# A polynomial-sketch attention and feed-forward kernel: its program rewritten as small named steps in a given order, with cheaper weight conversion, plain-maximum rounding grids and the first block's numerators ahead of its normalisation

## The chip, the core and the metric

The kernel runs on one core of a Trainium2 chip. The metric is the device time of one execution in microseconds (us), as the median of several runs. The program before takes 302.24 us (three runs, 301.96 to 303.37). The profile of one execution spans 299.0 us from its first to its last instruction.

A core has five engines that run their own instruction streams and wait for each other through semaphores. PE (TensorE) multiplies matrices and writes to PSUM, [...]. DVE (VectorE) and ACT (ScalarE) do elementwise work and copy results out of PSUM. POOL (GpSimd) does a little elementwise work on SBUF. SP (SyncE) issues the DMA transfers.

## The reference, cut to what matters

```python
def phi(x):                                   # x: (4, 4, 1088, 32)
    a = einsum('rd,bhsd->bhsr', S1, x)        # r = 8
    b = einsum('rd,bhsd->bhsr', S2, x)
    return outer(a, b).reshape(..., 64)
kv  = einsum('bhsf,bhsd->bhfd', phi(k), v)
z   = sum(phi(k), axis=2)
num = einsum('bhsf,bhfd->bhsd', phi(q), kv)
den = einsum('bhsf,bhf->bhs', phi(q), z) + 1e-6
x   = (num / den) laid out as (4352, 128)
out = ((x @ w1) * (x @ w2)) @ w3 @ w_out      # w1, w2: 128 x 1024, w3: 1024 x 1024, w_out: 1024 x 128
```

The denominator can come near zero, so it needs more than single precision. Both kernels get it from split numbers: a leading part rounded to a coarse grid plus a rest. They don't sum phi(k). They build the Gram matrix `G = k' k` (32 x 32 for each head), from it `T = G S1`, from it `N = P T` with `P = S2' S2`, and the denominator of a row is the product of its `a = q S1` and its `y = q N`. The sketch matrices and the four weights arrive as float64, as pairs of 32-bit words, and are converted to float32 on the chip. Both kernels use `w3o = w3 @ w_out`, computed once, so that each group of 512 rows needs three products for each of eight 128-column blocks c: a, b and o.

## The kernel before

It is a list of closures, merged by estimated costs. A weight is converted in chunks of 512 columns, with float64 words `lo` and `hi`:

```python
def words():                                   # ACT
    nc.scalar.mul(x["c"], hi.bitcast(F32), 2.0 ** -112)
    nc.scalar.mul(x["m"].bitcast(I32), lo.bitcast(U32), 2.0 ** -29)
    if signs:                                  # w1, w2 only
        x["s"] = zeros_with_signs(x["c"], 128, CW)
def join():                                    # DVE
    if signs:
        nc.vector.scalar_tensor_tensor(t, c, 3, x["s"], ALU.logical_shift_left, ALU.bitwise_or)
    else:
        nc.vector.tensor_scalar(t, c, 3, 0x7FFFFFF8, ALU.logical_shift_left, ALU.bitwise_and)
        nc.vector.scalar_tensor_tensor(t, c, -(1 << 31), t, ALU.bitwise_and, ALU.bitwise_or)
def add():                                     # DVE
    nc.vector.tensor_tensor(x["t"], x["t"], x["m"].bitcast(I32), ALU.add)
```

A rounding grid is the row maximum, cut to a power of two and scaled; then it is added and subtracted:

```python
def to_grid(m, bits):                          # two small DVE instructions for each grid
    nc.vector.tensor_scalar(mi, mi, 0x7F800000, None, ALU.bitwise_and)
    nc.vector.tensor_scalar(m, m, 1.5 * 2.0 ** (24 - bits), None, ALU.mult)
```

A batch b of k gives Gram and value sums that share one bank (`kvz`), and the rows past 1024 are a separate small set of products for pairs of batches. After them come G, T and N, each a product of split numbers (`pair_mm`, three matmuls). A half batch of q goes through these steps:

```python
# grid_q, lead_q (ACT, two passes), rest_q (POOL, or DVE where lean), ay1 and ay2 (a and y, PE), split, dens, dens2, phi ...
nc.vector.tensor_mul(bs, C, 1 / den)           # dens2: b is divided by the denominator
nc.vector.tensor_mul(ph, a x bs)               # phi: outer products, 128 x 1024
# phT: 8 PE transposes (L807), 2 ACT copies; nd: two matmuls with kv (L818); ACT copy to xT (L822)
```

The feed-forward of group g, block c:

```python
a_ps = psum.tile([128, 512], F32, tag="h", bufs=3)
nc.tensor.matmul(a_ps, w1[:, cols], xT[key])                     # L862
nc.scalar.copy(a_sb, a_ps)                                       # L864
b_ps = psum.tile([128, 512], F32, tag="h", bufs=3)
nc.tensor.matmul(b_ps, w2[:, cols], xT[key])                     # L866
nc.vector.tensor_mul(ab, a_sb, b_ps)                             # L868
nc.tensor.matmul(o_ps[g], w3o[:, c], ab, ...)                    # L875
```

The first part is written out in a fixed order, with 88 idle matmuls on zeros (L215) in it. From group 1 on, the streams are merged:

```python
run(merge(ffn_steps(1, 16), k_steps(1), w_out))
run(merge(ffn_steps(None, 4), q_main(1, 0)))
run(merge(ffn_steps(2, 6), q_main(1, 1), rest_steps(1) + k_steps(2)))
# ... cut ...
run(merge(ffn_steps(7, 6), q_rest()))
run(ffn_steps(8, 2))
```

Of the kernel before, what the change touches and what calls it, by code (L numbers as in the profile page):

```python
# [15 lines left out]
U32 = mybir.dt.uint32  # L16
I64 = mybir.dt.int64
# [4 lines left out]
EPS = 1e-6  # L22
CW = 512
LAG = 16
NRAW = 6


def bview(t, free):

    return bass.AP(tensor=t.tensor, offset=t.offset, ap=[list(t.ap[0])] + [list(d) for d in free])  # L30


@with_exitstack
def kernel(
    ctx: ExitStack,
    tc: tile.TileContext,
    q: bass.AP,
    k: bass.AP,
    v: bass.AP,
    S1: bass.AP,  # L40
    S2: bass.AP,
    moe_w1: bass.AP,
    moe_w2: bass.AP,
    moe_w3: bass.AP,
    moe_w_out: bass.AP,
    out: bass.AP,
):

    nc = tc.nc
    B, H, S, D = q.shape
    r = S1.shape[0]
    assert (B, H, S, D, r) == (4, 4, 1088, 32, 8)
    DM, DF = moe_w1.shape
    assert DM == H * D == 128 and DF % CW == 0  # L60
    NC = DF // 128
    NJ = S // 128
    SM = NJ * 128
    SR = S - SM
    HD = H * D
    NT = S // 32
    assert SR == 64 and NT * 32 == S
    KM = H * NJ * D

    consts = ctx.enter_context(tc.tile_pool(name="consts", bufs=1))  # L70
    io = ctx.enter_context(tc.tile_pool(name="io", bufs=2))
    work = ctx.enter_context(tc.tile_pool(name="work", bufs=2))
    psum = ctx.enter_context(tc.tile_pool(name="psum", bufs=1, space=bass.MemoryType.PSUM))

    def load_main(t, src, b):
        nc.sync.dma_start(t.rearrange("p h c d -> p h (c d)"),
                          bass.AP(tensor=src.tensor, offset=b * H * S * D,
                                  ap=[[NJ * D, 128], [S * D, H], [1, NJ * D]]))

    def load_rest(t, src, m):
        for i in range(2):  # L90
            nc.sync.dma_start(t[i * SR:(i + 1) * SR],
                              bass.AP(tensor=src.tensor, offset=((2 * m + i) * H * S + SM) * D,
                                      ap=[[D, SR], [S * D, H], [1, D]]))

    k_sb, v_sb, k_rs, k_all = {}, {}, {}, {}
    by_head = {}

    def load_in(which, b):


        src, held = {"k": (k, k_sb), "v": (v, v_sb)}[which]
        if which == "k":
            t = io.tile([128, KM + HD], F32, tag="k", name="k_sb")
            k_all[b] = t if b % 2 == 0 else t[:, :KM]
            held[b] = t[:, :KM].rearrange("p (h c d) -> p h c d", h=H, c=NJ)
        else:
            held[b] = io.tile([128, H, NJ, D], F32, tag=which, name=which + "_sb")
        if which == "v" and b:
            for t in range(4):
                nc.sync.dma_start(held[b][t * 32:(t + 1) * 32].rearrange("p h c d -> p h (c d)"),  # L110
                                  bass.AP(tensor=v.tensor, offset=b * H * S * D + t * NJ * D,
                                          ap=[[32 * D, 32], [S * D, H], [1, NJ * D]]))
        else:
            load_main(held[b], src, b)
        if which == "k" and b % 2 == 0:
            k_rs[b // 2] = t[:, KM:].rearrange("p (h d) -> p h d", h=H)
            load_rest(k_rs[b // 2], k, b // 2)

    def load_by_head(which, b):
        n = {"q": NT, "k": 32}[which] * D  # L120
        t = io.tile([128, n], F32, tag=which + "h", bufs={"q": 2, "k": 1}[which], name=which + "h")
        if which == "q":
            nc.sync.dma_start(t, bass.AP(tensor=q.tensor, offset=b * H * S * D, ap=[[n, 128], [1, n]]))
        else:
            for h in range(H):
                nc.sync.dma_start(t[h * 32:(h + 1) * 32],
                                  bass.AP(tensor=k.tensor, offset=(b * H + h) * S * D, ap=[[n, 32], [1, n]]))
        by_head[which, b] = t

    def natural(t, half):  # L130

        n = work.tile([128, 4, H, D], F32, tag="w3c", bufs=3, name="nat")
        nc.scalar.copy(n, bview(t[:, 0, 4 * half], [[D, 4], [NJ * D, H], [1, D]]))
        return n.rearrange("p c h d -> p c (h d)")

    qT_rest = consts.tile([128, B * SR], F32, tag="qT_rest")
    v_rs = [consts.tile([128, H, D], F32, tag=f"vr{m}", name=f"vr{m}") for m in range(2)]

    w1 = consts.tile([DM, DF], F32, tag="w1")
    w2 = consts.tile([DM, DF], F32, tag="w2")  # L140
    wo = consts.tile([128, NC, DM], F32, tag="wo")
    w3o = consts.tile([128, NC, DM], F32, tag="w3o")

    def chunk_src(name, i):
        if name == "wo":
            n = CW // DM
            return bass.AP(tensor=moe_w_out.tensor, offset=moe_w_out.offset + i * n * 128 * DM,
                           ap=[[DM, 128], [DM * 128, n], [1, DM]])
        if name == "w3":
            ko, half = divmod(i, DF // CW)  # L150
            return moe_w3[ko * 128:(ko + 1) * 128, half * CW:(half + 1) * CW]
        src = moe_w1 if name == "w1" else moe_w2
        return src[:, i * CW:(i + 1) * CW]

    NH = DF // CW
    chunks = [(w, i) for i in range(NH) for w in ("w1", "w2")]
    chunks += [("wo", i) for i in range(NC * DM // CW)] + [("w3", i) for i in range(NC * NH)]
    raw, n_raw = {}, [0]

    def load_raw(n):  # L160
        while n_raw[0] < min(n, len(chunks)):
            i = n_raw[0]
            n_raw[0] += 1
            raw[i] = io.tile([128, CW], I64, tag="raw", bufs=NRAW, name="raw")
            if i == 2:

                nc.vector.memset(raw[i].bitcast(I32)[:1, :1], 0)
            src = chunk_src(*chunks[i])
            dst = raw[i]
            if len(src.shape) == 3:  # L170
                dst = dst.rearrange("p (c d) -> p c d", d=DM)
            nc.sync.dma_start(dst, src)

    s_raw = consts.tile([r, 2, D], I64, tag="s_raw")
    for i, x in enumerate((S1, S2)):
        nc.sync.dma_start(s_raw[:, i], x)
    load_in("k", 0)
    load_in("v", 0)
    load_by_head("q", 0)
    load_rest(v_rs[0], v, 0)  # L180
    load_raw(2)

    def load_more():
        load_raw(NRAW)
        load_in("k", 1)
        load_by_head("k", 1)
        load_in("v", 1)
        load_by_head("q", 1)
        load_rest(v_rs[1], v, 1)

# [3 lines left out]
    make_identity(nc, ident)  # L194
    mask4 = consts.tile([128, H], F32, tag="mask4")
    mask2 = consts.tile([128, 2], F32, tag="mask2")
    for t in (mask4, mask2):
        nc.vector.memset(t, 0.0)
    for h in range(H):
        nc.vector.memset(mask4[h * D:(h + 1) * D, h:h + 1], 1.0)  # L200
        nc.vector.memset(mask2[h * D:(h + 1) * D, h % 2:h % 2 + 1], 1.0)
    mask4n = consts.tile([128, H], F32, tag="mask4n")
    nc.vector.tensor_scalar(mask4n, mask4, -1.0, None, ALU.mult)
    mask_blk = bview(mask4, [[1, H], [0, D]])
    first_act = consts.tile([1, 1], F32, tag="first_act")
    nc.scalar.copy(first_act, mask4[:1, :1])


    zeros = consts.tile([128, 256], BF16, tag="zeros")
    nc.vector.memset(zeros, 0.0)  # L210
    idle_ps = psum.tile([128, CW], F32, tag="out", name="idle_ps")

    def idle(times, n=256):
        for _ in range(times):
            nc.tensor.matmul(idle_ps[:, :n], zeros[:, :128], zeros[:, :n], start=True, stop=True)  # L215
    idle(24)
    sgn = [consts.tile([128, CW], I32, tag=f"sgn{i}", name=f"sgn{i}") for i in range(2)]
    for t in sgn:
        nc.vector.memset(t, 0)

    def halves(words, n):

        w = words.bitcast(I32)
        return bview(w, [[2, n]]), bview(w[:, 1:], [[2, n]])

    def zeros_with_signs(c, p, n):

        sgn.append(sgn.pop(0))  # L230
        t = sgn[0][:p, :n]
        nc.scalar.copy(bview(t.bitcast(F16)[:, 1:], [[2, n]]), c)
        return t

    def split_words(lo, hi, p, n):


# [10 lines left out]
        def parts():  # L248
# [4 lines left out]
            return a.bitcast(F32), m  # L253
        return words, parts

    def convert(n, dst, signs=True):

        x = {}
# [741 lines left out]
```

## Time and profile before

| what | value |
|---|---|
| time, median of three | 302.24 us |
| span of the profile | 299.0 us |
| first feed-forward matmul starts | 34.04 us |
| last matmul (the transposes of the last output) ends | 295.45 us |
| feed-forward matmuls a, b, o | 212 us of PE busy time |
| feed-forward on DVE (product a times b) | 47.1 us |
| bytes moved by DMA | 22.37 MB |

The page gives for each engine how long it had an instruction in work (busy), and the same cut into 40 slices. The matmul of a float32 operand has two records in the trace, so 72 products show as 144. The groups of instructions tell what one instruction of a kind and shape takes, and a table of windows gives the busy time of each engine in a stretch of the span. The chain of waits follows the last instruction back to what released it.

In the first 20 us PE is busy for 16.93 us, but many of these matmuls are the idle ones. From 80 to 280 us PE is busy in practically all of the time.

### The profile page before, as it was taken

The page shows a single profiled execution, that of the slowest core. Times are in us where ns is not written, and L with a number is a line of the kernel's source. Part 1 is how long each engine was busy: PE and PEld are TensorE (multiplying, and loading weights), DVE is VectorE, ACT ScalarE, POOL GpSimd, SP SyncE. Part 2 cuts the span into 40 slices and gives each one's busy share as a digit, 9 for nine tenths or more (in the row PEclk, how much of TensorE's full clock was granted, in tenths as well). Part 3 has the DMA queues.
Part 4 walks back from the last instruction along what each step waited for, and adds up shares of the span by engine and source line. Part 5 has one row for each costly group of instructions (what it writes and reads, how often), then busy time and mean ns, then how long its engine had stood idle before and what let it go on. Part 6 is the DMA issues. An engine that isn't in the chain of part 4 may idle for free.

```text
span 299.0 us, 5582 instructions
## 1 busy us (share of the span) xinstructions
PE 282.7 (95%) x2214; PEld 159.8 (53%) x2214; DVE 207.6 (69%) x523; ACT 117.1 (39%) x226; POOL 7.5 (3%) x12
## 2 busy tenths in 40 slices
PE   7987799589999999999999999999999999999994
PEld 5876343267767774545644435464444444444572
DVE  6989779999998985699579329864862583453131
ACT  4634665667886322320242322122423323223122
POOL 0000000000000010010010001000100000000000
PEclk9999999979999999999999999999999999999999
DMA  5649996456744002200100200020002002002020
GB/s 164 211 99 311 254 309 252 134 160 201 246 123 134 0 2 35 71 2 10 30 0 0 35 2 1 2 37 0 2 0 35 2 0 35 1 2 35 0 35 18
DMA packets 28729, 22.37 MB, mean 75 GB/s; under 512 B 20000, under 2 KB 25248, under 8 KB 28704
## 3 DMA queue, kind: packets, MB, share of 16 engines
q1 hardware_dynamic: 28704, 22.03, 26.8%
q8 instruction: 17, 0.28, 0.4%
q14 instruction: 8, 0.07, 0.1%
HBM read 19.80 MB, written 2.23 MB: 74 GB/s over the span
## 4 chain that ended last, share of the span: by engine, by line
PE 80%; DVE 11%; ACT 3%; DMA 2%; issue 1%; SPq 1%; DVEq 0%
PE ps_o L875 19%; PE a_ps L862 19%; PE b_ps L866 18%; PE ps_kvz L557 5%; PE ps_w3o L428 5%; PE ps_x L818 3%; PE ps_wt L421 2%; PE ps_c L725 2%; PE ps_ph L807 2%; DMA k_sb<-in_k_dram 1%; DMA raw<-in_moe_w_dram 1%; PE ps_ab L504 1%; DVE g_k L301 1%; DVE w3c L285 1%; PE ps_c L738 1%
## 5 line engine op out<-in xcount | busy, mean ns | idle before, releaser
L868 DVE TENSOR_TENSOR ab<-ffa,b_ps 128x512 f32<-128x512 f32 (+1 forms) x72 | 47.1, 655 | 64.7 <-PE b_ps L866 62.9
L864 ACT COPY ffa<-a_ps 128x512 f32<-128x512 f32 (+1 forms) x72 | 40.4, 562 | 98.1 <-PE a_ps L862 98.0
L862 PE MATMUL a_ps<-xT,w 128*128 128x512 f32 (+1 forms) x144 | 71.9, 581 | 1.0 <-ACT xT L822 0.7
L866 PE MATMUL b_ps<-xT,w 128*128 128x512 f32 (+1 forms) x144 | 70.3, 570 | 0.0
L875 PE MATMUL ps_o<-ab,w3o 128*128 128x512 f32 (+1 forms) x144 | 70.0, 582 | 0.1
L866 PEld LDWEIGHTS b_ps<-xT,w 128*128 128x128 f32 x144 | 27.2, 190 | 30.1 <-issue 24.9
L875 PEld LDWEIGHTS ps_o<-ab,w3o 128*128 128x128 f32 x144 | 25.3, 189 | 23.9 <-issue 21.6
L862 PEld LDWEIGHTS a_ps<-xT,w 128*128 128x128 f32 x144 | 24.9, 190 | 23.5 <-issue 14.3
L809 ACT COPY pT<-ps_ph 128x512 f32<-128x512 f32 (+1 forms) x18 | 9.2, 565 | 21.0 <-PE ps_ph L807 21.0
L428 PEld LDWEIGHTS ps_w3o<-wo,w3T 128*128 128x128 f32 x128 | 16.5, 205 | 1.5 <-issue 1.2
L428 PE MATMUL ps_w3o<-wo,w3T 128*128 128x128 f32 x128 | 17.0, 289 | 0.0
L269 ACT ACTIVATE cv_c<-raw 128x512 f32<-128x512 f32 x22 | 14.9, 679 | 2.9 <-DVE w3c L282 1.5
L270 ACT ACTIVATE cv_m<-raw 128x512 int32<-128x512 uint32 x22 | 15.0, 681 | 1.8 <-DVE w3c L285 1.5
L421 PE MATMUL ps_wt<-ident,w3c 128*128 128x128 f32 x64 | 10.2, 288 | 4.7 <-DVE w3c L285 4.7
L215 PE MATMUL idle_ps<-zeros 128*128 128x256 bf16 x88 | 12.7, 309 | 1.7 <-DVE zeros L210 1.7
L822 ACT COPY xT<-ps_x 128x512 f32<-128x512 f32 (+1 forms) x9 | 5.1, 563 | 19.0 <-PE ps_x L818 19.0
L421 PEld LDWEIGHTS ps_wt<-ident,w3c 128*128 128x128 f32 x64 | 7.5, 147 | 8.7 <-ACT cv_c L269 4.2
L215 PEld LDWEIGHTS <-zeros 128*128 128x128 bf16 x88 | 9.6, 112 | 3.8 <-DVE zeros L210 1.7
L701 POOL TENSOR_TENSOR q<-qT,q 128x512 f32<-128x512 f32 x5 | 5.9, 1183 | 208.6 <-ACT q L697 208.6
L423 ACT COPY w3T<-ps_wt 128x512 f32<-128x512 f32 x16 | 9.2, 585 | 4.9 <-PE ps_wt L421 4.6
L807 PEld LDWEIGHTS ps_ph<-ident,ph 128*128 128x128 f32 x68 | 7.9, 142 | 5.8 <-issue 4.0
L285 DVE CUSTOM_DVE_ANT_0 w3c<-w3c,cv_m 128x1024 uint16<-128x1024 uint16 x16 | 10.8, 682 | 0.0
(182 smaller groups left out, 343.9 us busy)
## 6 DMA issues: line engine op xcount, KB each, us to landing
raw<-in_moe_w_dram SPq DMA_DIRECT2D x20, 512.0 KB, 5.0
qh<-in_q_dram SPq DMA_DIRECT2D x4, 544.0 KB, 5.8
k_sb<-in_k_dram SPq DMA_DIRECT2D x4, 512.0 KB, 5.2
out_dram<-oT SPq DMA_DIRECT2D x32, 64.0 KB, 1.9
kh<-in_k_dram SPq DMA_DIRECT2D x12, 128.0 KB, 6.4
v_sb<-in_v_dram SPq DMA_DIRECT2D x12, 128.0 KB, 5.1
raw<-in_moe_w_out_dram SPq DMA_DIRECT2D x2, 512.0 KB, 7.7
v_sb<-in_v_dram SPq DMA_DIRECT2D x1, 512.0 KB, 4.9
```

The lines of the kernel that those rows point to most:

```text
L215: nc.tensor.matmul(idle_ps[:, :n], zeros[:, :128], zeros[:, :n], start=True, stop=True)
L269: nc.scalar.mul(x["c"], hi.bitcast(F32), 2.0 ** -112)
L270: nc.scalar.mul(x["m"].bitcast(I32), lo.bitcast(U32), 2.0 ** -29)
L421: nc.tensor.transpose(ps[:, c], w3c[i][:, c * 128:(c + 1) * 128], ident)
L428: nc.tensor.matmul(ps, w3T[ko][:, c], wo[:, c], start=(c == 0), stop=(c == NC - 1))
L557: nc.tensor.matmul(out[h * D:(h + 1) * D], lhs, rhs, start=start, stop=stop, skip_group_check=True)
L807: nc.tensor.transpose(ps[:, j * 128:(j + 1) * 128], s["ph"][:, j, 2 * p:2 * p + 2].rearrange("p h i j -> p (h i j)"), ident)
L862: nc.tensor.matmul(a_ps[:, :n], w1[:, cols], xT[key], start=True, stop=True)
L864: nc.scalar.copy(a_sb[:, :n], a_ps[:, :n])
L866: nc.tensor.matmul(b_ps[:, :n], w2[:, cols], xT[key], start=True, stop=True)
L868: nc.vector.tensor_mul(ab[:, :n], a_sb[:, :n], b_ps[:, :n])
L875: nc.tensor.matmul(o_ps[g][:, :n], w3o[:, c], ab_sb.pop((g, c))[:, :n], start=c == 0, stop=c == NC - 1)
```

## The change

The whole program is cut into named steps, and one list gives the order in which all of them are issued, so each engine's own order follows from it. The changes in the work itself:

- A weight is converted in tiles of 1024 columns. The float32 magnitude is built in one DVE instruction, and the low bits and the sign, which ACT writes as the two 16-bit halves of one word, are joined in one addition.
- A grid is the maximum itself times a power of two, no longer cut to a power of two. The scaling happens inside the instruction that adds, so the two small instructions are gone.
- Rows past 1024 are a ninth chunk of k and v, with zeros in the other half of the partitions. The value sums have a bank of their own and no longer share that of the Gram sums. G, T and N take two matmuls for each product.
- The first 512 rows of q form their outer products and numerators from the undivided b, before N is there. The denominator divides the numerators, which are then transposed. Only this first block does so.
- Only the first two blocks of q take the form with few large matmuls for a and y (before: three). The rest of q is subtracted on DVE instead of POOL; for batch 0 POOL forms the outer products of k.
- 24 idle matmuls instead of 88. The buffers of `ab` go from 18 to 17, those of k, v and q from two to one each.

```diff
-        nc.scalar.mul(x["c"], hi.bitcast(F32), 2.0 ** -112)
-        nc.scalar.mul(x["m"].bitcast(I32), lo.bitcast(U32), 2.0 ** -29)
+    act.mul(x["c"], halves(raw[n], 1024)[1].bitcast(F32), 2.0 ** -112)                                   # step w.c
+    act.copy(bview(sign_bits[n % 2].bitcast(F16)[:, 1:], [[2, 1024]]), x["c"])                           # step w.s
+    act.mul(bview(sign_bits[n % 2].bitcast(U16), [[2, 1024]]), halves(raw[n], 1024)[0].bitcast(U32), 2.0 ** -29)  # w.m
-            nc.vector.tensor_scalar(t, c, 3, 0x7FFFFFF8, ALU.logical_shift_left, ALU.bitwise_and)
-            nc.vector.scalar_tensor_tensor(t, c, -(1 << 31), t, ALU.bitwise_and, ALU.bitwise_or)
-        nc.vector.tensor_tensor(x["t"], x["t"], x["m"].bitcast(I32), ALU.add)
+    dve.tensor_scalar(x["d"].bitcast(I32), c, 3, 0x7FFFFFF8, ALU.logical_shift_left, ALU.bitwise_and)    # step w.j
+    dve.tensor_tensor(d, d, sign_bits[n % 2], ALU.add)                                                   # step w.a
 ... cut ...
-        nc.vector.tensor_scalar(mi, mi, 0x7F800000, None, ALU.bitwise_and)
-        nc.vector.tensor_scalar(m, m, 1.5 * 2.0 ** (24 - bits), None, ALU.mult)
+        eng.scalar_tensor_tensor(dst, m, 2.0 ** (24 - bits), x, ALU.mult, ALU.add)
+        eng.scalar_tensor_tensor(dst, m, -2.0 ** (24 - bits), t, ALU.mult, ALU.add)
 ... cut ...
-                ps = psum.tile([128, 128], F32, tag="kvz", name="ps_kvz")
+                    a["g"] = ps("kvz", [128, 2 * D], "ps_g")
+                    a["kv"] = ps("out" if b == 0 else "t", [128, 64], "ps_kv")
 ... cut: first block of q (kind "A") ...
+            bsrc = s["Cb"].rearrange("p j (h i) -> p (j h) i", i=r) if cut else s["bs"]
+                        pe.matmul(o[:, j, 64 * p:64 * (p + 1)], s["pT"][:, p, j * 128:(j + 1) * 128],
+                                  kz[b][:, 64 * p:64 * (p + 1)], start=True, stop=True)
+                dve.tensor_mul(s["xs"]..., s["x"]..., bview(s["rc"], [[1, nj * H], [0, D]]))
+                    pe.transpose(cols(t, j), s["xs"][:, j], ident)
 ... cut: the order, its first part ...
+ORDER = """
+s.load c.mask k0.zero k0.load1 k0.load0 k0.loadr s.zero c.ident kr0.load q0.load s.words kr1.load s.pair w1.load
+s.split k0.nat0 kh1.load kr0.tr s.lead k0.tr0 s.T k0.kT0 k0.max0 kr0.kT k0.nat1 s.blk k0.g0 q0.tr kr0.ab kr1.tr
 ... cut ...
+k0.N1 q0.sca k0.kv0 k0.Na w0.m k0.kv1 k0.Nb k0.kvr k0.Nf k0.Nh k0.Nl q0.C1 k0.kvm w0.j q1.l2 k0.kzt q0.A1 warm0
+q0.smy w3.c q0.al q0.sty q0.C1t q0.shy q0.phi q1.l1 k0.kz q0.sly q0.pt0 q0.scy q0.p01 q0.pt1 q0.pc0 q0.p2 q1.A0
+w0.a q0.pc1 q0.x q0.p12 q1.rm q0.dn q1.C0 q0.de w1.j q0.rc q0.xs w1.a q0.xt q0.xT w3.j w3.s g0.0a q0.restT
 ... cut ...
```

In the step names, k0 is batch 0 of k, q0 and q1 are the first two blocks of q, w0 and w1 hold the first and second half of w1 and w2, w2 is w_out, w3 to w10 are w3, f is the fold of w3 and w_out, and g is the feed-forward with its steps a, c (copy), b, m (product) and o.

## The prediction

> **What bounds the kernel now.** I read the page's shares first, then the slices, then a table of windows, and last the groups of instructions.
>
> ```profile
> PE 282.7 (95%) x2214; PEld 159.8 (53%) x2214; DVE 207.6 (69%) x523; ACT 117.1 (39%) x226; POOL 7.5 (3%) x12
> ...
> PE   7987799589999999999999999999999999999994
> ```
>
> PE is busy for 95% of the span, but the slices show where it isn't: the first 60 us and the last slice. From the ninth slice on it never pauses. The windows (us; busy of PE, weight loads, DVE, ACT, POOL; granted clock; DMA) put numbers to that:
>
> ```profile
> 20.00:34.00 14.00, 11.01 (x84) 8.22 (x84) 13.07 (x39) 6.63 (x11) 0.00 (x0) 1.00 1.03 272
> 34.00:42.00 8.00, 7.46 (x32) 4.10 (x32) 5.40 (x13) 6.14 (x11) 0.00 (x0) 1.00 1.10 271
> 42.00:60.00 18.00, 14.10 (x41) 5.95 (x40) 16.95 (x35) 11.46 (x21) 0.00 (x0) 1.00 0.63 227
> 60.00:80.00 20.00, 18.66 (x206) 14.34 (x206) 19.08 (x33) 15.34 (x29) 0.00 (x0) 0.91 0.65 191
> 80.00:115.00 35.00, 34.91 (x352) 25.15 (x349) 32.11 (x93) 18.28 (x35) 1.16 (x1) 1.00 0.25 76
> ...
> 280.00:299.00 19.00, 14.74 (x57) 10.12 (x55) 3.67 (x8) 3.58 (x9) 0.00 (x0) 1.00 0.10 21
> ```
>
> So there are three stages. In the **head**, up to the first feed-forward matmul at 34.04 us, the chain of waits runs mostly through DVE (13.07 of 14 us busy). In the **conversion stage**, 34 to 80 us, PE idles 0.54 + 3.90 + 1.34 = 5.8 us while DVE is nearly full. After that PE is the bound until its last matmul ends at 295.45 us. The output's last copies and its transfer take the remaining 3.55 us.
>
> What fills DVE are the conversions, and what they cost is in the groups (busy us, mean ns of one, idle before):
>
> ```profile
> L270 ACT ACTIVATE cv_m<-raw 128x512 int32<-128x512 uint32 x22 | 15.0, 681 | 1.8 <-DVE w3c L285 1.5
> ...
> L285 DVE CUSTOM_DVE_ANT_0 w3c<-w3c,cv_m 128x1024 uint16<-128x1024 uint16 x16 | 10.8, 682 | 0.0
> L282 DVE SCALAR_TENSOR_TENSOR w3c<-cv_c,w3c 128x512 int32<-128x512 int32 x16 | 10.8, 679 | 0.0
> ...
> L281 DVE TENSOR_SCALAR w3c<-cv_c 128x512 int32<-128x512 int32 x16 | 6.4, 419 | 0.0
> ...
> L296 DVE TENSOR_SCALAR g_pair<-g_pair 128x1 int32<-128x1 int32 x13 | 2.0, 152 | 0.3
> L297 DVE TENSOR_SCALAR g_pair<-g_pair 128x1 f32<-128x1 f32 x13 | 2.0, 152 | 0.3
> ...
> L701 POOL TENSOR_TENSOR q<-qT,q 128x512 f32<-128x512 f32 x5 | 5.9, 1183 | 208.6 <-ACT q L697 208.6
> ```
>
> [...] 419 ns for the tensor_scalar of 512, 679 for the one with two tensors. So replacing such a two-tensor operation is worth more than its count. [...] a 128x1 grid step still takes 152 ns. [...] the first 24 idle matmuls of 256 columns took 5.04 us, 0.21 each, and 13 later ones 1.58 us, 0.12 each. After PE's pause up to 59 us the granted clock is 0.62 from 60 to 64 us.
>
> **DVE, part by part.** Conversions before: 4 chunks x (0.68 + 0.69) = 5.5 us and 18 x (0.42 + 0.68 + 0.68) = 32.0, together 37.5. After: 11 tiles x (0.81 for a tensor_scalar of 1024, as the split of k takes + 1.3 for the addition, twice 0.68 less a fixed part) = 23.2. Saved: 14. Grid steps before: pairs 26 x 0.15, q 18 x 0.145, a and y 16 x 0.18, k 8 x 0.14, sketch 2 x 0.16, or 10.8 us; five small ones stay: saved 10. The subtraction of q's rest comes from POOL: plus 5 x 0.69 + 0.4 = 3.9. Batch 0's outer products go to POOL: minus 2 x 1.21 and 0.4 for a rest. Sum: about 23 us less. The durations on DVE sum to 229 us before (they overlap; busy is 207.6), so 206 after.
>
> **ACT.** Before: 22 x (0.68 + 0.68) + 4 x 0.77 = 33.0 us. After: 11 x (1.2 + 1.3 + 1.2) = 40.7, as every tile now needs its signs from ACT. Plus 8 us, on an engine that was busy for 39.6 of the 60 us from 20 to 80, and for 15.34 of 20 in its fullest window. I take it as hidden.
>
> **The head.** In the new order DVE needs the sketch (0.6 + 1.6 us after its words at 3.4), one maximum, the block form of the sketch (PE's small transposes wait for a transfer of 128-byte pieces, whose like landed at 6.4 us in the old trace; so about 7.7), q's transposition (q landed some 6 us after its issue; here it stands before v in the queue, so about 8), then maxima, leads and rests of k and a few more: 7 us, until about 15.2. Before, the maximum of the Gram sums stood at 15.93. From it the list has 22 steps up to the last part of N and the value mask, 8.1 us by the old durations, then 20 steps to the division of the numerators, 9.6 us, among them 0.81 + 1.3 + 0.81 us of weight conversion. Less 1 us for overlap, plus 1.4 for PE's transposes and ACT's copy: 33.3 us. PE isn't warmed at the start any more; if its 24 idle matmuls run at half clock (5.1 us) the first outer products are transposed later, and it is about 35. I take **34.2**, no gain against 34.04. What is gained lies elsewhere: by then w1 and w2 are wholly converted (before, two of four chunks came later, 2.7 us of DVE), and PE has done the second block's a and y.
>
> **PE after the first feed-forward matmul.** Before: 295.45 - 34.04 = 261.4 us. The a, b, o work, the fold and the transposes are unchanged. Gone: the second block's a and y, 0.28 + 2.0 us (35.9 to 38.6), now in the head; the third such block as quarters, 1.5 (1.23 for one block's 40 records of c in the chain, and 0.3) instead of 2.3 us: 0.8; per batch of k the separate rest (0.77 us) against one more chunk (16 records at 14.5 ns, 0.24; 128 records took 1.85 us from 10.75 to 12.96 without the products between), and G, T, N with four matmuls for six (1.2 us before, I estimate 0.8): 0.9 x 3 = 2.7. Sum -5.8 us. Of the 5.8 us of idle time I expect 4 to stay, -1.8: until group 1 starts the list has some 31 us of DVE durations (27 busy, by the ratio 229 to 207.6) beside 28 us of PE work, so neither hides the other with ease. The clock: 0.09 x 20 us lost before, I expect 0.5 to stay: -1.3. So 261.4 - 5.8 - 1.8 - 1.3 = 252.5.
>
> **The sum.** 34.2 + 252.5 + 3.55 for the end = 290.3 us of span, plus 3.2 by which the time exceeds the span: **293.5 us**, 2.9% less than 302.24.
>
> **Rivals.** (1) *The conversion stage stays bound by DVE.* The list places one product of a feed-forward block among 3 to 4 us of other DVE work, in strict order, and PE has three banks for a and b. Summed from the first feed-forward step to that of group 2, DVE has 87 us of durations, some 79 busy, and PE some 87 to 90. That speaks for PE, narrowly. If order makes them wait in turn, 5 to 10 us of PE idle come on top: 299 to 303. (2) *The head is longer.* DMA bunches (w1 before v, single buffers) or POOL's products of k, 2.4 us each by the 1183 ns for 512, hold up the numerators, or the cold PE does. [...] It would add 2 to 4 us, straight to the end. (3) *The schedule is as good as its making suggests.* If DVE's 23 us really free PE in the conversion stage and the head loses its gaps, PE idles 1 us, the head ends at 32: 288 or lower. (4) *All DVE savings are hidden*: PE still sets everything after 80 us, where DVE's share is no matter; then only the PE terms count, -5.8, and the time is 296.4.
>
> **Range and chances.** The terms that I trust are PE's -5.8. The head is uncertain by 2 us either way, the idle time by 4, with a longer tail upwards. So 286 to 301 should hold it eight times in ten. The 2% border is 296.2, not 3 us from my value: faster 0.63, within 2% 0.29, slower 0.08.
>
> **What would show it.** The first feed-forward matmul at 33 to 36 us; PE idle of about 4 us from there to 80, spread in short waits on DVE's product of a and b or ACT's copies instead of the one pause at 56 to 59; DVE busy near 186 us, ACT near 125; no DVE group of grid steps but for k; conversions at 0.81 and 1.3 us; PE full from 80 us on; from the first feed-forward matmul to PE's last about 252 us. I am wrong if the first feed-forward matmul comes after 37 us, if PE idles over 9 us behind it, if the granted clock falls again, or if small products among large ones cost PE more than before.

## The result and the profile after

The changed kernel takes **288.68 us** (median of six, 285.28 to 292.94) against 302.1 us for the kernel before beside it: a ratio of 0.953, 95% interval 0.947 to 0.959. The ratio leaves out two of the six, 289.94 and 292.94 us, as having run at a lowered clock (0.988 and 0.973), but that clock belongs to what the head of this kernel does, and with all six the medians stand at 0.956. The profile is of the execution at 285.28 us, the shortest; why it is not the typical one is the main finding below.

The page of the changed kernel, its shares and slices (busy tenths of PE and the granted clock, 40 slices of 7.1 us):

```profile
PE 267.2 (94%) x2166; PEld 153.8 (54%) x2166; DVE 177.4 (63%) x418; ACT 120.6 (43%) x196; POOL 8.7 (3%) x34
...
PE   1889989999998999899999999999999999999993
...
PEclk9997999999999999999999999999999999999999
```

From the second slice on PE is busy for 80% or more of every slice but the last; before, that was so from the ninth on. The clock falls once before the end, in the fourth slice. The windows of the changed kernel (us; busy of PE, weight loads, DVE, ACT, POOL; clock; DMA share, GB/s):

```profile
20.00:34.00 14.00, 12.72 (x174) 11.40 (x175) 12.45 (x43) 9.81 (x12) 2.42 (x3) 0.88 0.47 156
34.00:42.00 8.00, 7.29 (x46) 3.93 (x46) 7.35 (x14) 6.08 (x7) 0.00 (x0) 1.00 0.52 197
42.00:60.00 18.00, 17.43 (x208) 10.28 (x206) 17.73 (x36) 16.34 (x23) 0.40 (x2) 1.00 0.81 290
60.00:80.00 20.00, 20.00 (x169) 12.94 (x169) 16.02 (x34) 15.69 (x22) 0.00 (x0) 1.00 0.66 188
80.00:115.00 35.00, 32.56 (x614) 23.92 (x612) 29.15 (x62) 17.23 (x29) 1.56 (x4) 1.00 0.17 45
```

From 42 to 80 us PE idles 0.57 us, where the kernel before idled 5.2 (3.90 + 1.34), and its clock stays at 1.00. The 2.4 us missing from 80 to 115 are two gaps put down to "issue" in the middle of runs of small products; nothing in the trace is waited for there. The groups that answer to the conversions shown of before (busy us, mean ns of one, idle before):

```profile
L317 DVE TENSOR_SCALAR w3c<-cv_c 128x1024 int32<-128x1024 int32 x8 | 5.5, 687 | 0.0
L322 DVE CUSTOM_DVE_ANT_0 w3c<-w3c,sg 128x2048 uint16<-128x2048 uint16 x8 | 9.8, 1228 | 1.0 <-ACT sg L306 1.0
L306 ACT ACTIVATE sg<-raw 128x1024 uint16<-128x1024 uint32 x11 | 15.1, 1376 | 1.4 <-DMA raw<-in_moe_w_dram 1.4
L480 POOL TENSOR_TENSOR kp<-kab 128x1024 f32<-128x1024 f32 x2 | 4.0, 1984 | 7.7 <-ACT kab L511 7.7
```

I cut each execution at the first feed-forward matmul. What lies ahead is the head; the **rest** runs from there to the end of the last matmul. The end behind it is about 3.6 us in all of them. One profile per kernel:

| kernel | median, range (us) | profiled execution (us) | first feed-forward matmul | rest |
|---|---|---|---|---|
| before | 302.1, 300.6 to 303.4 | span 299.0 | 34.04 | 261.4 |
| changed | 288.68, 285.28 to 292.94 | 285.28 | 36.56 | 243.3 |
| changed, again | 290.04, 286.15 to 291.24 | 289.73 | 41.43 | 242.9 |
| old conversion | 293.10, 292.89 to 296.82 | 292.89 | 38.65 | 248.9 |
| before, new conversion | 305.11, 304.83 to 306.42 | 304.94 | 34.19 | 265.4 |
| grid steps back | 293.69, 292.39 to 293.88 | 293.78 | 43.19 | 245.2 |
| warm start | 289.89, 285.98 to 291.28 | 291.28 | 42.56 | 243.3 |
| G_a early | **285.30**, 284.83 to 285.71 | 284.83 | 36.72 | 242.7 |
| G_a late | 289.52, 288.33 to 291.47 | 290.20 | 41.00 | 243.8 |
| kp on DVE | 290.85, 290.11 to 292.25 | 291.33 | 42.24 | 243.5 |
| idle matmuls in gaps | 284.05, 283.04 to 290.93 | 290.93 | 44.20 | 241.3 |
| numerators behind N | 292.21, 288.73 to 294.02 | 292.47 | 42.84 | 244.2 |
| one bank | 286.19, 285.33 to 288.90 | 286.02 | 36.84 | 243.8 |
| put together | 287.83, 286.23 to 292.40 | 287.23 | 38.60 | 243.3 |

The rest stays between 241.3 and 244.2 us in every version of the changed kernel but those that add DVE work (old conversion, grid steps). The head moves by up to 7.6 us.

### The profile page after: what moved, and what is told of

Its sections match the earlier page's. It is cut to its first block, busy times and chain, and to the rows that moved or that the text cites. A ratio compares the mean times of both kernels' runs of the same rounds, so it can differ in the third digit from the quotient of the medians.

```text
span 283.5 us, 5335 instructions
## 1 busy us (share of the span) xinstructions
PE 267.2 (94%) x2166; PEld 153.8 (54%) x2166; DVE 177.4 (63%) x418; ACT 120.6 (43%) x196; POOL 8.7 (3%) x34
## 4 chain that ended last, share of the span: by engine, by line
PE 91%; ACT 3%; DVE 2%; issue 1%; DMA 1%; ACTq 0%; DVEq 0%
PE b_ps L1073 21%; PE a_ps L1063 21%; PE ps_o L1085 21%; PE ps_w3o L347 5%; PE ps_g L457 4%; PE ps_c L775 3%; PE ps_x L1029 3%; PE ps_wt L337 2%; PE ps_ph L984 2%; PE ps_kv L555 2%; PE ps_ab L530 1%; PE idle_ps L167 1%; ACT sg L302 1%; DMA s_raw<-in_S_dram 1%; PE ps_xt L1003 1%
## 5 line engine op out<-in xcount | busy, mean ns | idle before, releaser
L1063 PE MATMUL a_ps<-xT,w 128*128 128x512 f32 (+1 forms) x144 | 68.6, 574 | 0.7 <-ACT xT L1021 0.7
L1085 PE MATMUL ps_o<-ab,w3o 128*128 128x512 f32 (+1 forms) x144 | 67.1, 572 | 0.0
L1085 PEld LDWEIGHTS ps_o<-ab,w3o 128*128 128x128 f32 x144 | 26.3, 190 | 23.9 <-issue 22.6
L347 PEld LDWEIGHTS ps_w3o<-wo,w3T 128*128 128x128 f32 x128 | 15.2, 192 | 2.8 <-issue 1.7
L306 ACT ACTIVATE sg<-raw 128x1024 uint16<-128x1024 uint32 x11 | 15.1, 1376 | 1.4 <-DMA raw<-in_moe_w_dram 1.4
L990 ACT COPY pT<-ps_ph 128x512 f32<-128x512 f32 (+1 forms) x18 | 10.1, 572 | 11.4 <-PE ps_ph L984 11.4
L302 ACT CAST sg<-cv_c 128x1024 f16<-128x1024 f32 x11 | 14.9, 1363 | 0.0
L298 ACT ACTIVATE cv_c<-raw 128x1024 f32<-128x1024 f32 x11 | 12.5, 1150 | 0.0
L457 PE MATMUL ps_g<-kk 128*32 128x64 f32 x288 | 10.4, 233 | 1.2 <-issue 1.2
L457 PEld LDWEIGHTS ps_g<-kk 128*32 128x32 f32 x288 | 8.8, 114 | 4.0 <-issue 2.1
L322 DVE CUSTOM_DVE_ANT_0 w3c<-w3c,sg 128x2048 uint16<-128x2048 uint16 x8 | 9.8, 1228 | 1.0 <-ACT sg L306 1.0
L984 PE MATMUL ps_ph<-ident,ph 128*128 128x128 f32 x68 | 10.0, 273 | 0.0
L457 PE MATMUL ps_g<-k,kk 128*32 128x32 f32 x288 | 9.9, 201 | 0.0
```

The costliest lines, as they stand in the source:

```text
L298: act.mul(x["c"], halves(raw[n], 1024)[1].bitcast(F32), 2.0 ** -112)
L302: act.copy(bview(sign_bits[n % 2].bitcast(F16)[:, 1:], [[2, 1024]]), x["c"])
L306: act.mul(bview(sign_bits[n % 2].bitcast(U16), [[2, 1024]]), halves(raw[n], 1024)[0].bitcast(U32), 2.0 ** -29)
L347: pe.matmul(t["o"], w3T[ko][:, c], wo[:, c], start=c == 0, stop=c == NC - 1)
L457: pe.matmul(o[h * D:(h + 1) * D], lhs, rhs, start=start, stop=stop, skip_group_check=True)
L984: pe.transpose(t[:, j * 128:(j + 1) * 128], ph_cols(j, p), ident)
```

## The experiments

### Where the gain comes from: the conversion, in both orders

The changed kernel with the old conversion (third DVE operation back, no copy of the signs on ACT):

```diff
-    act.copy(bview(sign_bits...), x["c"])                      # w.s
-    act.mul(bview(sign_bits.bitcast(U16)...), lo, 2.0 ** -29)  # w.m
+    act.mul(sign_bits, lo, 2.0 ** -29)
     dve.tensor_scalar(d, c, 3, 0x7FFFFFF8, ...)                # w.j
+    dve.scalar_tensor_tensor(d, c, -(1 << 31), d, ALU.bitwise_and, ALU.bitwise_or)
```

> The changed kernel with the weight conversion of the kernel before: three VectorE operations for each of the 11 weight tiles instead of two, and two ScalarE operations instead of three. It gives VectorE back some 11 times 1.2 us = 13 us between 20 and 80 us, and takes 11 times 1.36 us = 15 us off ScalarE. Theory A (the conversion stage was bound by VectorE, and the lighter conversion freed it): VectorE was busy 33.7 of the 38 us from 42 to 80 us already, so the stage grows; TensorE's idle time from its first feed-forward matmul to 80 us goes from 0.6 us to 5 or more, and the time rises by 5 to 9 us, to about 294 to 298. Theory B (the new order alone brought the gain, and VectorE's savings lay beside TensorE's work): the time stays within 1.5 us of 288.7, and TensorE stays without idle time up to 80 us.

This is a little more than the old conversion: w1 and w2 had two DVE operations for a tile before and get three here, which puts 2 x 1.23 us more into the head. It took 293.10 us; the rest grew from 243.3 to 248.9 us. The waits of PE from 38.7 to 80 us (total, times, longest), and the last window:

```profile
PE ps_wt L339 <- DVE w3c L324: 1.0, 1, 1.0
...
PE b_ps L1075 <- ACT w3T L343: 0.7, 1, 0.7
PE ps_g L459 <- DVE kk L451: 0.5, 1, 0.5
```
```profile
60.00:80.00 20.00, 18.04 (x146) 10.05 (x145) 19.01 (x33) 12.07 (x19) 0.00 (x0) 1.00 0.72 181
```

DVE is full again (19.01 of 20 us), and PE waits for it. Theory A holds in kind. In size the time rose by 4.4 us, a little under its 5 to 9, and PE's waits up to 80 us are 2.6 us, not 5; one more wait for a conversion, of 0.7 us, ends at 106 us. Of the 5.5 us by which the rest is longer, 2.8 are such waits; the others are not tied to a wait.

The reverse, the kernel before with only the conversion changed:

```diff
-    nc.scalar.mul(x["m"].bitcast(I32), lo.bitcast(U32), 2.0 ** -29)
+    x["s"] = zeros_with_signs(x["c"], 128, CW)
+    nc.scalar.mul(bview(x["s"].bitcast(U16), [[2, CW]]), lo.bitcast(U32), 2.0 ** -29)
-    nc.vector.scalar_tensor_tensor(t, c, -(1 << 31), t, ALU.bitwise_and, ALU.bitwise_or)
```

> The kernel before with nothing changed but its weight conversion: a tile's low words are written as 16-bit numbers under the sign bits, so that VectorE does two operations for a tile instead of three and ScalarE three instead of two. Theory A (the conversion stage was bound by VectorE): the 5.8 us that TensorE idles between its first feed-forward matmul and 80 us go down to about 2, the clock's fall at 60 us goes with them, and the time goes from 302 to 296 to 298. Theory B (the order brought the gain): ScalarE's longer work takes the place of VectorE's, TensorE idles as long as before, and the time stays within 1.5 us of 302.

It is *slower* than before: ratio 1.0125 (1.0075 to 1.0174). PE's waits from 34 to 115 us, of this kernel:

```profile
PE ps_wt L416 <- DVE g_k L292: 2.1, 1, 2.1
PE ps_w3o L423 <- ACT w3T L418: 1.6, 4, 0.6
PE ps_wt L416 <- DVE w3c L280: 1.4, 1, 1.4
PE a_ps L857 <- ACT ffa L859: 0.9, 2, 0.5
```

DVE fell from 16.95 to 13.94 of the 18 us up to 60. Yet PE idled 5.8 us from its first feed-forward matmul to 80 us, as long as before (5.7), and ACT was busy for 18.54 of 20 us from 60 to 80. What became of the time that DVE won is seen in front of the long pause. First the kernel before, from the timelines of ACT, DVE and PE (start, duration, engine):

```profile
52.95 0.69 ACT L269 ACTIVATE cv_c<-raw 128x512 f32<-128x512 f32 x1
53.52 0.68 ACT L270 ACTIVATE cv_m<-raw 128x512 int32<-128x512 uint32 x1
54.08 0.59 ACT L864 COPY ffa<-a_ps 128x512 f32<-128x512 f32 x1
...
54.70 0.69 DVE L868 TENSOR_TENSOR ab<-ffa,b_ps 128x512 f32<-128x512 f32 x1 [0.28 <-ACT ffa L864]
...
59.26 0.63 PE L421 MATMUL ps_wt<-ident,w3c 128*128 128x128 f32 x4 [3.20 <-DVE w3c L285]
```

then the same place with the new conversion:

```profile
53.50 0.67 ACT L269 ACTIVATE cv_c<-raw 128x512 f32<-128x512 f32 x1
54.20 0.77 ACT L233 CAST sgn<-cv_c 128x512 f16<-128x512 f32 x1
54.84 0.76 ACT L271 ACTIVATE sgn<-raw 128x512 uint16<-128x512 uint32 x1
55.48 0.55 ACT L859 COPY ffa<-a_ps 128x512 f32<-128x512 f32 x1
...
56.06 0.69 DVE L863 TENSOR_TENSOR ab<-ffa,b_ps 128x512 f32<-128x512 f32 x1 [3.34 <-ACT ffa L859]
...
59.26 0.66 PE L416 MATMUL ps_wt<-ident,w3c 128*128 128x128 f32 x4 [2.06 <-DVE g_k L292]
```

In DVE's order its product of a and b stands ahead of this conversion of w3, and it waits for ACT's copy of a. That copy came at 55.48 instead of 54.08 us (0.55 us of this were late already, the third ACT pass ahead of it is the rest). DVE, done earlier with less work, stood idle for 3.34 us, and PE's transposes of w3 started at 59.26 us in both kernels. So the theory with the right mechanism is B (ACT's longer work takes the place of DVE's), though the time rose by 3 us and so left its 1.5. The conversion doesn't do it alone: the order and the other differences bring 9 us (302.25 to 293.10: a rest 12.5 us shorter, a head 4.6 us longer), and the light conversion another 4.4 in the new order (293.10 to 288.68), while in the old one it costs 3.

### Where the time still goes: the head

Idle matmuls at the start, as before:

```diff
-ORDER: s.load c.mask ...
+ORDER: c.zeros warm1 s.load c.mask ...        # warm1: 24 idle matmuls
```

> The changed kernel with 24 idle matmuls at the very start, as the kernel before has them. Theory A (the head was 2.4 us longer than predicted because TensorE came cold into the Gram products, 4.35 us for 144 of them): the Gram products take about 2.2 us, the Gram maximum starts at about 16.7 us instead of 18.9, the first feed-forward matmul at 34 to 34.8 us instead of 36.6, and the time falls by 1.5 to 2.5 us to about 286.5. Theory B (the head is set by VectorE, the products on GpSimd and the transfers): the Gram products get shorter, but the first feed-forward matmul stays within 0.5 us of 36.6.

Neither theory came true. The median is 289.89, and the profiled head ended at 42.56 us. The clock was at 0.50 from 10 to 20 us, so the Gram products took 5.5 us and gained nothing; and in the chain stood a 128x32 operation, G_a, that took 1.97 us, where the changed kernel's first profile has 0.18. That led to the next four runs. First the unchanged changed kernel once more:

> The changed kernel once more, for a second profile and more times. Its profiled execution at 285.3 us was the shortest of its runs, the others were at 288 to 289. If the difference lies in the head (a small VectorE operation held up for 1.9 us behind a product on GpSimd, as it was with 24 idle matmuls at the start, or TensorE at half rate for longer), a profile of an execution at 288 to 289 us shows its first feed-forward matmul at 39 to 40 us, and from there to the last matmul again 243 to 244 us. If it lies in the rest, the first feed-forward matmul stays at 36.6 us.

The timelines of POOL and DVE, first of the execution at 285.28 us, then of the one at 289.73 us (start, duration, engine):

```profile
20.48 2.01 POOL L480 TENSOR_TENSOR kp<-kab 128x1024 f32<-128x1024 f32 x1 [2.07 <-ACT kab L511]
...
20.50 0.18 DVE L128 SCALAR_TENSOR_TENSOR G_a<-G_g,G_t 128x32 f32<-128x32 f32 x1
```
```profile
21.22 1.95 POOL L480 TENSOR_TENSOR kp<-kab 128x1024 f32<-128x1024 f32 x1 [1.50 <-ACT kab L511]
...
21.24 1.98 DVE L128 SCALAR_TENSOR_TENSOR G_a<-G_g,G_t 128x32 f32<-128x32 f32 x1
```

In both the two operations start within 0.02 us of each other. In the first G_a took 0.18 us, and the product took 2.01 us instead of 1.95. In the second G_a took 1.98 us, up to 23.22, and the product had ended at 23.17: DVE waited the whole product out. What decides between the two cases the traces don't show: by the recorded starts GpSimd was 0.02 us ahead both times. PE waited 2.6 us for G_a, up to 23.4 us, and within that wait, at 22.5 us, the clock fell from 1.00 to 0.50. The windows behind it, of the second execution:

```profile
24.00:28.00 4.00, 4.00 (x20) 3.85 (x18) 2.58 (x11) 2.95 (x3) 0.00 (x0) 0.50 0.96 285
28.00:32.00 4.00, 4.00 (x98) 3.46 (x98) 2.18 (x11) 0.72 (x2) 0.00 (x0) 0.50 0.07 18
32.00:36.00 4.00, 4.00 (x41) 3.53 (x38) 3.78 (x11) 2.19 (x4) 0.00 (x0) 0.91 0.02 4
```

Half rate lasted from 22.5 to 32.75 us, against 23.9 to 27.3 in the first execution. The head ends 4.87 us later, at 41.43 us where 39 to 40 had been expected, and the rest is the same (242.9 against 243.3).

The granted clock on record for each execution gives an estimate of how long it ran at half rate, also where there is no profile: 2 x (1 - clock) x span, as each fall in these traces goes to 0.50. For the two profiled executions of the changed kernel it gives 3.4 and 10.4 us, and their traces show 3.41 and 10.24. For the ten executions of the changed kernel this estimate gives 3.4 us twice (times 285.28 and 286.15), about 7 four times (287.85 to 289.94), 10.4 three times (289.73 to 291.24) and 15.7 once (292.94). So the times follow the half rate, in steps of some 3.4 us of it; only the steps of 3.4 and 10.4 have a profile. Then G_a moved by one word in the list, to end before the product starts, and to start within it:

```diff
-... k0.Gt q0.sma q1.max k0.abc1 k0.Ga k0.kp1 q0.sta ...
+... k0.Gt q0.sma k0.Ga q1.max k0.abc1 k0.kp1 q0.sta ...     # G_a early
+... k0.Gt q0.sma q1.max k0.abc1 k0.kp1 q0.sta k0.Ga ...     # G_a late
```

> The changed kernel with one small VectorE operation of the head, the rounded Gram block G_a, ahead of the maximum of the second query block instead of behind it; it is then done some 0.6 us before the second product of batch 0's k starts on GpSimd. Theory A (in some executions G_a, which reads two tiles of SBUF, starts just behind that product, waits it out for 1.9 us, and TensorE then idles long enough to fall to half rate): G_a takes 0.1 us, no operation of the head waits for GpSimd, the first feed-forward matmul comes at 36 to 36.6 us, and the median falls by 1.5 to 3 us against the changed kernel, to about 286. Theory B (the spread has another cause): the median stays within 0.7 us of the changed kernel's.

> The changed kernel with the rounded Gram block G_a one VectorE operation later than in the change (behind s_t), so that it always starts inside the second product of batch 0's k on GpSimd; s_t, which reads one tile of SBUF and one of PSUM, comes ahead of it and starts inside that product too. Theory A (an operation that reads two tiles of SBUF waits the GpSimd product out, one that reads one does not; the gap on TensorE then costs half rate for about 10 us): s_t takes 0.2 us, G_a 1.5 to 1.9 us, the first feed-forward matmul comes at 41 to 42 us in every execution, and all times lie at 289 to 291.5. Theory B (the order of these two does not matter): times spread from 285 to 290 as those of the changed kernel.

Early: 285.30 us, all four executions within 0.9 us and none with more than 5.7 us at half rate by the same estimate (5.7 for the profiled one, whose trace shows 3.41), ratio to before 0.944 (0.941 to 0.947); measured beside it, the changed kernel stood at 290.04. G_a took 0.17 us from 20.1 us on, and the product started at 20.63. Late: 289.52, none under 288.33. The timeline of DVE of the late version:

```profile
21.05 0.27 DVE L123 SCALAR_TENSOR_TENSOR s_t<-s_ga,ps_a 128x128 f32<-128x128 f32 x1
21.25 1.78 DVE L126 SCALAR_TENSOR_TENSOR G_a<-G_g,G_t 128x32 f32<-128x32 f32 x1
```

The product ran from 21.03 to 22.98. s_t, with one input in SBUF and one in PSUM, started within it and took 0.27 us; G_a, with both in SBUF, took 1.78 us, to the product's end. Theory A holds for the early version; its gain of 4.7 us (3.4 against the first median) is larger than expected. For the late version it holds in the profile and in kind: two of its times lie below the expected 289, and their clock of 0.988 stands for some 7 us at half rate, not 10.

The products off GpSimd altogether, in DVE's wait for the Gram products:

```diff
-                    k_phi(f["kp", half], x[:, 0], x[:, 1], pool)
+                    k_phi(f["kp", half], x[:, 0], x[:, 1], dve)     # and k0.ab1 ahead of k0.gram0 on PE
```

> The changed kernel with batch 0's two large products of k on VectorE instead of GpSimd, in the 2.8 us that VectorE waits for the Gram products, and their sketch products ahead of the Gram products on TensorE. It takes the kp product of 2 us, whose end the value sums wait for, off GpSimd, and with it every chance of a VectorE operation waiting for GpSimd there; it puts 1 us of TensorE's work ahead of the Gram products. Theory A (the hand-over to GpSimd is what spreads the times): the Gram maximum comes 0.5 to 1 us later, at about 19.7 us, the first feed-forward matmul at 36 to 37 us, and the median falls by 1 to 2.5 us against the changed kernel's. Theory B (VectorE's time is what the head lacks): it lengthens by the 2.7 us of the two products, and the median rises by 1 to 3 us.

290.85 us. No operation waits for GpSimd any more, yet the head ends at 42.24: the Gram maximum came at 21.57 us (the extra PE work took 1.9 us, where the first profile has 1.08 for eight such records, the Gram products 5.16 instead of 4.35), PE waited 1.8 us for G_a, and half rate ran from 24.2 to 34.4. So neither theory fits, and the run suggests that the wait on GpSimd matters through the gap on PE, and that another gap does the same. The sharper test of that takes the filler out of a gap (with G_a early):

```diff
-... k0.T1 q0.C0 k1.kT0 k0.Ta ... k0.N0 ... k0.N1 ...
+... k0.T1 k1.kT0 k0.Ta ... k0.N0 ... k0.N1 q0.C0 ...
```

> The kernel with G_a early (285.3 us), and the first block's numerators behind the products N again instead of ahead of them: it undoes the part of the change that put the first numerators ahead of N. TensorE then has nothing between the sketched Gram block T, at about 21.5 us, and N, some 2 us later, when VectorE has split T. Theory A (a gap of 2 us on TensorE in the head halves its rate for about 10 us): clock 0.50 from 24 to about 34 us, first feed-forward matmul at 40 to 42 us, time 289 to 291. Theory B (only the numerators' own time moves, off one stretch and on to another): N comes 0.3 us earlier, the numerators' 1.9 us behind it delay the value sums, first feed-forward matmul at 37 to 38.5 us, time 285.5 to 287.

292.21 us. PE's waits from 20 to 30 us, and two windows:

```profile
PE ps_N L676 <- DVE T_p L657: 2.1, 1, 2.1
```
```profile
24.00:28.00 4.00, 2.38 (x11) 2.35 (x11) 1.86 (x9) 3.97 (x4) 0.91 (x3) 0.50 0.55 178
28.00:32.00 4.00, 4.00 (x80) 3.88 (x83) 1.45 (x9) 0.28 (x1) 0.00 (x0) 0.50 0.41 129
```

The gap of 2.1 us runs from 23.6 to 25.6, half rate from 23.8 to 34.0. The fall came 0.2 us into the gap, and with G_a early the clock fell too, at 24.6, but for 3.4 us only; so the gap can have added to the length of the half rate, but need not have started it. From the Gram maximum to the first feed-forward matmul 42.84 - 20.97 = 21.9 us passed instead of 36.72 - 19.05 = 17.7. (Another 1.9 us of this profile are a later Gram maximum, as one of the k transfers landed later.) So the first numerators ahead of N are worth about 4 us. Their own duration is 1.8 us, and the rest fits the longer half rate; the two were not separated.

Filling the gaps, and the version put together:

```diff
+ORDER: c.zeros warm1 ... s.T warm2 ... warm3 kr1.tr ... warm4 k0.T0 ...    # 24, 8, 12, 10 idle matmuls
```

> The changed kernel with idle matmuls at the start (24) and in three gaps of the head in which TensorE waits (8, 12 and 10 of them), about 1 us each at full rate. With idle matmuls at the start alone the clock granted fell to 0.50 from 10 to 20 us, behind the two gaps of 7.3 to 10.3 us. Theory A (a gap in TensorE's work of 1 to 3 us costs half rate for the 5 to 10 us behind it): without the gaps the clock stays at 1.00 through the head, the Gram products take about 2.2 us, the first feed-forward matmul comes at 34 to 35 us, and the time is 285 to 287. Theory B (the fall follows the work done at the start, not the gaps): the clock falls as it did, and the time stays at 288 to 291.

> A version put together from the runs: the changed kernel with G_a early, idle matmuls at the start and in three gaps of the head, the ScalarE table load directly behind the issue of the sketch's load (1.28 us that otherwise stand between the load's landing and its conversion), and the second block's numerators behind the transposes of the first block's quotients. From the single ones: the idle matmuls gave fast executions at 283.0 to 284.4 against 285.3 for G_a early alone; the table load is 1.2 us ahead of the sketch, the transposes 0.5 us. If these add, the first feed-forward matmul comes at 33 to 34.5 us and the time is 282 to 283.5; if the head is set by the transfers of the k rows, which landed at 10 us, the table load brings nothing, and it is 283.5 to 284.5.

With the gaps filled three of four executions took 283.0 to 284.4 us, the shortest of all runs. The profile is of the fourth, at 290.93: PE stood 3.3 us in the head for nothing that the profile shows,

```profile
PE ps_a L784 <- issue: 3.3, 1, 3.3
```

and half rate ran from 21.9 to 35.6, after a first fall from 8.3 to 11.7. No profile shows one of the three good ones; their granted clocks of 1.000, 0.992 and 0.991 stand for 0 to 5 us at half rate, against 18 in the profiled one (17.1 by its trace). The version put together disappoints, 287.83 us: the clock fell from 13.25 to 20.1 us, right on the Gram products (5.55 us), and again from 37.1 to 40.6 behind a wait of 1.4 us. Why idle matmuls at the start are followed by that fall is open. The best version with narrow times is G_a early.

### Two parts of the change that matter less

The grid steps put back (two operations without effect behind each maximum):

```diff
+        eng.tensor_scalar(m.bitcast(I32), m.bitcast(I32), -1, None, ALU.bitwise_and)
+        eng.tensor_scalar(m, m, 1.0, None, ALU.mult)
```

> The changed kernel with two small operations without effect on the values put back behind each maximum of the sketch products, the queries and the k rows, as many as the kernel before has there: about 40 small ones of roughly 0.1 us, 4 to 6 us of VectorE. Theory A (VectorE is on the path in the head and in the conversion stage, and nowhere later): the head grows by 8 operations in its chain, 0.6 to 1.0 us, and the time by 0.5 to 1.5 us. Theory B (VectorE's time counts everywhere): the time grows by 4 us or more. Theory C (all of it is hidden): within 0.3 us.

There were 67 of them, and DVE's busy time rose by 11.6 us, twice what I had counted. The time is 293.69. The rest grew by 1.9 us, and the head is 1.8 us longer than in the second profile of the changed kernel. One added operation of 128x16 ran into the same GpSimd product:

```profile
21.17 0.17 DVE L125 TENSOR_SCALAR s_ga<-s_ga 128x16 int32<-128x16 int32 x1
21.38 1.86 DVE L126 TENSOR_SCALAR s_ga<-s_ga 128x16 f32<-128x16 f32 x1
```

The second has a single input and took 1.86 us, up to 23.24, while the product ran from 21.25 to 23.20; so two inputs in SBUF are not the only case of such a wait. The first started 0.08 us before the product and took 0.17. The number of theory B, 4 us or more, came true, but not its mechanism, that DVE's time counts everywhere: of 11.6 us some 4 to 5 reach the time, part of them in the head, where PE waited 3.7 us for G_a.

The value sums in the Gram bank again (with G_a early):

```diff
-                    a["kv"] = ps("out" if b == 0 else "t", [128, 64], "ps_kv")
+                    a["kv"] = a["all"][:, 2 * D:]      # and k3.gram0, k3.gram1 behind k2.kvm
```

> The kernel with G_a early (285.3 us), and the value sums again in the bank of the Gram products, with the Gram products of the last batch behind the value sums of the one before, which the shared bank demands: it undoes the own bank of the value sums. Theory A (the own bank lets the scheduler place the Gram products freely, but TensorE has enough other work): TensorE stays full behind 80 us, the time stays within 1 us of 285.3. Theory B (the bank is what kept the stretches together): each of the three later batches waits about 1 us for the bank, 2 to 4 us in all, and the time is 287 to 289.

286.19 us; the ratio's interval (0.943 to 0.957) overlaps that of G_a early. The rest is 1.1 us longer. The own bank brings about 1 us, by one profile, which is not clear of the spread of the times.

## Why the prediction was right, and where its steps were not

The time lies in the range and the sign is right, but the value was 4.8 us too high. Its errors have opposite signs, so that it came this near is partly luck: the rest was put 9.2 us too long, the head 2.4 us (first profile) or 7.2 (second) too short, and the 3.2 us "by which the time exceeds the span" compared a median with a single profile; in one and the same execution the two differ by about 1.8 us (1.7 to 2.1 in all runs).

**The rest: 252.5 predicted, 243.3 measured.** Terms are compared by adding, for each group of matmuls, the distances from one start to the next; that gives 261.1 and 243.1 us. Pauses of over 0.15 us are taken out of the groups and counted by themselves.

- *a and y of q, -3.1 predicted*: 12.9 to 9.2, so -3.7. In it, the second block's numerators went into the head (1.8 us, 33.63 to 35.45), where the prediction named them and gave them no time.
- *k, G, T, N, -2.7 predicted*: Gram and value products 12.8 to 9.1, T and N 3.5 to 2.2, a and b of k 3.0 to 2.7; -5.3. The two-matmul form was under-rated, and so was the ninth chunk in place of the separate rest.
- *Idle time, "I expect 4 to stay, -1.8"*: **this step failed.** PE's waits from its first feed-forward matmul to 80 us fell from 5.7 us to 0.6, so -5.1. The estimate weighed summed durations of DVE against PE's and found that neither hides the other. The runs show that the new order and the other differences take the waits to 2.6 us even with the old conversion, that the lighter conversion takes the rest, and that DVE then has slack: 16.02 busy of 20 us from 60 to 80. (That PE never pauses from the ninth slice on was misread, too: one of the old pauses, 1.20 us up to 61.09, lies in that slice.)
- *Clock, -1.3*: 0.38 x 4 + 0.05 x 4 = 1.7 us lost before from 60 to 68 us, none after. This lies in the transposes and the fold of w3, which took 2.0 us less.
- *Not in the prediction*: -3.3 in the feed-forward matmuls, which are equal work (428 to 414 ns from start to start for the output matmul), and -0.9 in smaller groups. Against all this stand the two pauses put down to "issue", +2.4, whose cause is open.

Most of the 3.3 us can be found in the trace. Where feed-forward matmuls follow each other, a record of 512 columns starts 429 ns after the one before it. The last record ahead of a run of small products (Gram, values, a and y, numerators) mostly takes 522, the first one behind such a run 533. So a pair of records takes 0.96 us in these lines of the kernel before, where value products stand on either side, and 0.86 elsewhere (53.32 to 54.18):

```profile
88.14 1.13 PE L862 MATMUL a_ps<-xT,w 128*128 128x512 f32 x2
89.10 1.02 PE L866 MATMUL b_ps<-xT,w 128*128 128x512 f32 x2
90.06 0.85 PE L557 MATMUL ps_kvz<-kkr 64*32 64x64 f32 x24
```

The kernel before has 75 records at such a border, the changed one 36, as its list bunches the small products. Summed, that is 3.0 us. Small products among large ones did matter, then, but the other way round from the sign that the prediction gave.

**The head: 34.2 predicted, 36.56 in the first profile, 41.43 in the second.** The step that failed is the Gram maximum "at about 15.2 us". It came at 18.90. DVE was done with all ahead of it at 16.1 us and then waited 2.8 us for PE: the 5.3 us of small PE products from 9.25 to 14.53 and the Gram products of 4.35 us ran at half rate until 17.0 us (eight records of a and b of k take 1.81 us from 10.77 and 1.08 from 18.91, eight Gram records 0.32 us up to 17.0 and 0.18 behind it). The prediction counted DVE's chain and took PE's as given. From the maximum on its working held: 34.2 - 15.2 = 19.0 predicted, 36.56 - 18.90 = 17.7 measured. Rival 2, the longer head, was therefore the true one, with its two causes named, cold PE and GpSimd; and GpSimd hurt not by its duration (2.4 us estimated, 1.95 to 2.01 measured) but by G_a's wait for its end, 1.98 us in the second profile, for which the prediction had no measured figure. Two signs of being wrong occurred, both in the head: "if the granted clock falls again", and, in the second profile (41.43), "if the first feed-forward matmul comes after 37 us". In the rest rival 3, the good schedule, came true.

**DVE and ACT.** DVE busy 177.4 against 186 predicted, ACT 120.6 against 125. The conversion's first operation took 687 ns, not 810, the addition 1228 as against 1300; ACT's three passes 42.5 us in place of 40.7, and hidden, as assumed, in the new order only.

## What to carry to other kernels

A time that spreads is worth two profiles: put the first point where they part beside the last point where they agree, and look for two operations that start within some hundredths of a microsecond of each other. In a stretch where TensorE isn't the bound, its gaps still count when half rate follows them: here an operation of 0.2 us on VectorE that took 1.98 us beside a GpSimd product came with 10.24 us at half rate instead of 3.41, and with a head 4.87 us longer. And work moved from one engine to another helps only where the order leaves the second one room: the same conversion brought 4.4 us in one order and cost 3 in the other, because the first engine then waited for the second.

## What the runs showed of the hardware

- Half rate in the head came in pieces of 3.41 us (first profile of the changed kernel, G_a early, one bank, and once beside a longer piece in each of the two versions with filled gaps), 6.83 (put together), 10.24 us (six profiles in which PE had waited 1.8 to 3.7 us in one piece) and 13.65 us once, with the 3.3 us. These are one, two, three and four times 3.41. The smallest of these six waits, 1.8 us, is that of kp on DVE. Half rate lasted while PE was busy: in the second profile of the changed kernel for 4.00 of 4 us from 24 to 28 us and from 28 to 32, at a clock of 0.50, which was back at 1.00 only at 32.75.
- The longest gap doesn't settle it alone. With idle matmuls at the start, 10.24 us came at 10.1 us with no gap over 1.1 us near it. With gaps of 0.8 and 0.2 us the clock fell in the changed kernel and not in the one with the old conversion. What decides was not shown.
- The granted clock reads 1.00 at the start of the changed kernel, while eight Gram records take 0.32 us up to 17.0 us and 0.18 behind it. That half rate is seen in the durations alone.
